# A dynamic convolution in front of a squared-ReLU layer on one core: the short conv form from block 5 instead of block 8

## The chip, the core and the metric

The kernel runs on one core of one Trainium2 chip. The metric is the device time of one launch in microseconds (us). The core has TensorE (PE in the profile; PEld is its weight load), VectorE (DVE), ScalarE (ACT), GpSimd (POOL) and SyncE (SP). Each works through its own list of instructions in order; they wait for each other by semaphores. Transfers (DMA) are issued here from the queues of SyncE and GpSimd.

## The reference

`x` is 8 x 4096 x 192, `weight_gen` 8 x 4096 x 8 x 7 (8 heads, 7 taps). The kernel may take the products in f16.

```
w = exp(weight_gen - max); w = w / sum(w)          # softmax over the 7 taps
y[s, h, :] = sum over k of w[s, h, k] * x_padded[s + k, h, :]   # 24 channels a head
h = maximum(y @ w_in, 0)                            # 192 -> 2048
out = (h * h) @ w_out                               # 2048 -> 192, for 32768 tokens
```

## The kernel before

**Blocks.** The 32768 tokens are 64 stretches of 512. Block 0 and block 1 hold one stretch each, blocks 2 to 32 two each (`BLOCKS`). The text counts blocks from 0 as the code does, so the sixth block is block 5. Each batch of the input is 8 stretches; block 5 is the first block of batch 1.

**What a block needs.** First the softmax weights of its tokens (class `Softmax`: `exp` on ScalarE, L244; sums, reciprocals and products on VectorE, L251, L258, L266). A part of the tokens is done in two to four pieces, each a step "S" in the plan. When a part's last piece is done, its rows are moved by DMA into tiles `wr` that lie by token: `move_rows` straight from SBUF (L361) for small parts, or through a copy `vd` in HBM (L280, then L327). Then VectorE multiplies `wr` with a mask into bands `bd` (L406; a step "B" for one stretch, in one or two instructions). The tokens of `x` come in as `xt` from GpSimd's queue, which also casts them to f16 (L317 to L327).

**The conv** of block j + 1 (step "C", `st_conv`) is a set of small matmuls of `xt` with `bd` into two PSUM tiles `yp`, which are then copied to `y` in SBUF. In the older form (L536) groups of 32 channels are computed in two rounds, since a group reaches over two heads: 120 matmuls, and ScalarE copies 1024 and 512 columns (L547). In the short form (`st_conv_spread`, L502) each head has its own 32 rows, so 80 matmuls are enough. The rows then hold 24 channels of one head, and heads 6 and 7 are brought into the 8 free rows by four DMAs `y<-y` (L516). Here 1024 columns are copied on ScalarE and 1024 on VectorE (L512). The channels of `y` then stand in another order, so `w_in` is needed with its rows in that order: `w_p`, loaded by `load_w_spread` (16 DMAs on GpSimd's queue, which cast) and completed by `cross_w_spread` (2 DMAs).

**The units.** A block has 16 units "u" (`st_unit`, units 0 to 15). One is six matmuls of `w_i` or `w_p` with `y` into a PSUM tile `h` (L581), the relu on ScalarE (L595), and, for two units at once, the square on VectorE (L599; units 14 and 15 one by one).

**The second product.** "M" is one half of a quarter of the block before: 64 matmuls of `g` with `w_o` (L630) into the PSUM tiles `o0` and `o1`, of which there is one each. Every second M ends a quarter: ScalarE copies one (L644), VectorE adds the other (L646), and the next M needs both free.

**The order** is written out by hand, and nothing reorders it: `plans` gives the steps of blocks 0 to 3; from block 4 on a string of steps is used, `steady` up to block 6 and `steady_spread` from block 7 (the block before the first that uses the short form).

```python
steady = "MuMuuu" * 3 + "MuuuMCu"
steady_spread = "MuMuuu" * 2 + "MuCMuuu" + "MuMuuu"
```

Softmax pieces (`TIMES`: block and unit), exps (`exp_time`) and bands (`us`) are put ahead of a unit. In blocks 4, 5 and 6 the two bands of the next block stand ahead of units 7 and 9, 5 and 9, 7 and 9; from block 7 on ahead of 1 and 5.

**Buffers** that bear on this: three PSUM tiles for `h` and `yp` together, three tiles `t` of two units each between ScalarE and VectorE, two `y`, two `xt`, two `o_sb`.

Of the kernel before, what the change touches and what calls it, by code (L numbers as in the profile page):

```python
# [9 lines left out]
def kernel(  # L10
# [26 lines left out]
    nc = tc.nc  # L37
# [7 lines left out]
    HK = H * KK  # L45
    G = D // H
    SPREAD = H - 2
    FIRST_SPREAD = 8
    HP = H // 2

    P = 128
# [11 lines left out]
    RT = 64  # L63
    NK = D // RT
# [34 lines left out]
    FIRST = 8  # L99
# [44 lines left out]
    def load_w_spread():  # L144

        def rows(head, k=None):
            a = moe_w_in[G * head : G * (head + 1)]
            return a if k is None else a.rearrange("(r k) c -> k r c", k=NK)[k]

        for e in (0, 1):  # L150
            for k in range(NK):
                for a, n, src in (
                    (0, G, rows(2 * k + e)), (G, RT // 2 - G, rows(SPREAD + e, k))
                ):
                    if k < 2:
                        p0 = RT * k + 32 * e + a
                        nc.gpsimd.dma_start(
                            out=w_p[p0 : p0 + n, :, 0, 0:NQ],
                            in_=src.rearrange("r (q c) -> r q c", q=WQ),
                        )  # L160
                    else:
                        for half in (0, 1):
                            p0 = RT * half + 32 * e + a
                            nc.gpsimd.dma_start(
                                out=w_p[p0 : p0 + n, :, 0, NQ:],
                                in_=src.rearrange("r (q h c) -> h r q c", q=WQ, h=2)[half],
                            )
    def cross_w_spread():
        for r0, r1 in ((0, RT), (RT, 0)):
            nc.gpsimd.dma_start(out=w_p[r0 : r0 + RT, :, 1], in_=w_p[r1 : r1 + RT, :, 0])  # L170
# [137 lines left out]
    def tile_start(j, i):  # L308

        t1 = (j % NBB + 1) * TB  # L310
        return TB - P if i == NT - 1 and t1 in ends(j // NBB) else starts[i]
# [169 lines left out]
    def st_conv_spread(j):  # L481

        s0, n = BLOCKS[j]
        y = p_y.tile([P, NK + 1, TB], f16, name="y")
        y_t[j] = y
        for ks in ((NK, NK - 1), (0, 1)):
            yp = ps_h.tile([P, 2, TB], f32, name="yp", tag="h")
            k0 = min(ks)
            for k in ks:
                for i in range(NT):  # L490
                    a, b = bounds[i], bounds[i + 1]
                    for half in (0, 1):
                        s = s0 + half
                        hi = a + (STEP if tile_start(s, i) == starts[i] else b - a)
                        bd = bd_t[s][:, H * a : H * hi].rearrange(
                            "p (g c e) -> p g e c", g=HP, e=2
                        )
                        for e in (0, 1):
                            head = 2 * k + e
                            p0 = RT * half + 32 * e  # L500
                            c0 = min(G * head, D - 32)
                            nc.tensor.matmul(  # L502
                                out=yp[p0 : p0 + 32, k - k0, a:b],
                                lhsT=x_t[s][:, i, c0 : c0 + 32],
                                rhs=bd[:, head // 2, e, 0 : b - a],
                                start=True,
                                stop=True,
                                skip_group_check=True,
                                tile_position=(0, p0),
                            )  # L510
            copy = nc.vector.tensor_copy if k0 == 0 else nc.scalar.copy
            copy(out=y[:, k0 : k0 + 2], in_=yp)  # L512
        for p0 in range(0, P, 32):
            head = SPREAD + p0 // 32 % 2
            r0 = p0 + G * head - min(G * head, D - 32)
            nc.sync.dma_start(out=y[p0 + G : p0 + 32, 0:NK], in_=y[r0 : r0 + G, NK])  # L516

    def st_conv(j):

        if j >= FIRST_SPREAD:  # L520
            return st_conv_spread(j)
# [49 lines left out]
    def st_unit(j, u):  # L571

        w = w_p if j >= FIRST_SPREAD else w_i
        h = ps_h.tile([P, 2, TB], f32, name="h", tag="h")
# [91 lines left out]
    with nc.allow_low_precision("fp16 matmul pipeline"), tc.manual_schedule():  # L666

        block_of = {n: j for j, (s, c) in enumerate(BLOCKS) for n in range(s, s + c)}
        parts = []
# [7 lines left out]
        def move_rows(s, engines=(nc.sync, nc.gpsimd)):  # L677

            n = parts.index(s)
            first = s.b * NBB + s.t0 // TB  # L680
            near = [p for p in parts[max(n - 1, 0) : n + 1] if p.b == s.b]
            for j in range(first, first + P * s.r // TB):
                wr_load_sbuf(j, near, range(NT), engines)
# [70 lines left out]


        steady = "MuMuuu" * 3 + "MuuuMCu"
        steady_spread = "MuMuuu" * 2 + "MuCMuuu" + "MuMuuu"
        plans = {
            0: "u B1 u u u E1 C S1 u u M u u",
# [9 lines left out]
        def at(j, u, kind, *args):  # L769
            fill.setdefault((j, u), []).append((kind, *args))  # L770
# [4 lines left out]
        TIMES = {  # L775
            (1, 0): ((3, 15), (4, 0)),
            (1, 1): ((4, 15), (5, 0)),
            (1, 2): ((4, 2), (5, 1), (5, 15)),
            (2, 0): ((6, 1), (6, 15), (7, 0)),
            (2, 1): ((7, 9), (8, 9)),  # L780
            (3, 0): ((9, 9), (10, 0), (10, 9), (11, 9)),
        }

        def exp_time(j, u):

            if u == 0:
                return j - 1, 12
            return j, {1: 0, 2: 1, 7: 3, 8: 4, 9: 4, 13: 12, 15: 8}[u]
# [17 lines left out]
            at(times[0][0] - 1, 0, "L", n)  # L806
        for j in range(len(plans), NBLK - 1):
            a = BLOCKS[j + 1][0]
            small = [p for p in parts if p.fb <= j + 1][-1].r == FIRST
            us = {4: (7, 9), 6: (7, 9)}.get(j, (5, 9) if small else (1, 5))  # L810
            if j + 1 >= FIRST_SPREAD:
                us = (1, 5)
            for n, u in enumerate(us):
                at(j, u, "B", a + n)
        for j in range(len(plans), NBLK):
            plan, u = [], 0
            for step in steady_spread if j + 1 >= FIRST_SPREAD else steady:
                if step == "u":
                    plan += [f"{kind}{n}" for kind, n in fill.get((j, u), ())]
                    u += 1  # L820
                plan.append(step)
            plans[j] = " ".join(plan)
# [14 lines left out]
        def soft(s):  # L837
            lo, hi = next(s.softs)
            s.total(lo, hi)
            s.recip(lo, hi)  # L840
            s.scale(lo, hi, nc.vector)
            if hi < s.rh:
                return
            if s.r == FIRST:
                move_rows(s)
                after = parts[parts.index(s) + 1]
                if after.b == s.b and after.r > FIRST:
                    s.store(nc.sync)
            else:
                s.store(nc.sync)  # L850
                stored.add(s)
                for w in [w for w in waiting if w[0] is s]:
                    waiting.remove(w)
                    load_rows(w[1])
# [21 lines left out]
        for j in range(NBLK):  # L876
            if j + 2 < NBLK:
                load_rows(j + 2)
            if j == 1:
                for q in range(WQ):  # L880
                    cross_w_in(q)
            u = 0
            for step in plans[j].split():
                kind, n = step[0], int(step[1:] or 0)
                if kind == "u":
                    st_unit(j, u)
                    u += 1
                elif kind == "M":
                    next(mm2)
                elif kind == "C" and j + 1 < NBLK:  # L890
                    st_conv(j + 1)
                    if j == 0:
                        x_load(3)
                    elif j + 2 < NBLK:
                        for k in range(BLOCKS[j + 2][0], sum(BLOCKS[j + 2])):
                            x_load(k)
                    if j == 5:
                        load_w_spread()
                    elif j == 6:
                        cross_w_spread()  # L900
                elif kind == "E":
                    parts[n].exp(*next(parts[n].exps))
                elif kind == "S":
                    soft(parts[n])
                elif kind == "B":
                    st_bands(n)
                elif kind == "L":
                    parts[n].load(nc.sync)


        j = NBLK - 1
# [44 lines left out]
```

## Time and profile before

| what | value |
| --- | --- |
| median of 3 runs | 730.38 us (729.42, 730.40, 730.38) |
| profiled execution, span | 728.4 us |
| mean granted TensorE clock | 1.000 |
| VectorE, ScalarE busy | 86%, 84% of the span |
| L581 matmuls, w_i and w_p | 576 and 2400, 376 ns each |
| L536 conv, older form | 6 convs of 120 matmuls |
| L502 conv, short form | 25 convs of 80 matmuls |

The profile is one execution of the program. Its span runs from the first to the last instruction; for the profiled execution no other time is given, and the runs' times lie 1.0 to 2.0 us above the span. Busy time is the time in which an engine works on at least one instruction. Durations of instructions that follow each other on one engine overlap a little, so that the cost of one in a chain is the distance from its start to the next one's. TensorE's work is read best from start to start too, because its ends are modelled.

The stretches between the first M of one block and of the next, from the view of busy time in chosen windows:

| block | from, to (us) | length | VectorE busy | ScalarE busy |
| --- | --- | --- | --- | --- |
| 4 | 73.28, 96.12 | 22.84 | 21.69 | 20.21 |
| 5 | 96.12, 118.69 | 22.57 | 21.21 | 19.38 |
| 6 | 118.69, 141.24 | 22.55 | 19.20 | 20.10 |
| 7 | 141.24, 163.33 | 22.09 | 21.05 | 18.52 |
| 8 | 163.33, 185.43 | 22.10 | 19.83 | 18.88 |

### The profile page before, as it was taken

What the parts mean: (1) busy time and instruction counts of PE and PEld (TensorE: products, weight loads), DVE (VectorE), ACT (ScalarE), POOL (GpSimd) and SP (SyncE); (2) the same over time, 40 slices, a digit from 0 to 9 for tenths busy, and PEclk for the clock granted to TensorE, in tenths of its full rate; (3) what the DMA queues carried; (4) which work ended last, traced back from release to release, by engine and by line L of the source; (5) the groups of instructions that cost most, each with busy time, mean ns of one, the idle gap of its engine ahead of it and who ended that gap; (6) DMA issues with size and microseconds to landing.
All of it is one profiled execution on the core that took longest, in us unless ns stands there. A gap on an engine that the chain in (4) does not pass through costs nothing.

```text
span 728.4 us, 31046 instructions
## 1 busy us (share of the span) xinstructions
PE 722.0 (99%) x14078; PEld 530.1 (73%) x14078; DVE 625.8 (86%) x839; ACT 612.0 (84%) x731; POOL 98.5 (14%) x146
## 2 busy tenths in 40 slices
PE   8999999999999999999999999999999999999998
PEld 5668877777777777777777777777777777777777
DVE  7999997998898998888988888988888988778753
ACT  6998888888888888888888888888888888888883
POOL 7231223411001100011001010010000110001000
PEclk9999999999999999999999999999999999999999
DMA  9664465676245443356432554343544325444112
GB/s 193 128 113 106 82 125 89 128 142 138 78 71 133 99 84 68 75 116 125 83 62 58 135 104 88 66 74 110 114 78 87 57 53 117 67 87 77 30 46 67
DMA packets 126272, 68.30 MB, mean 94 GB/s; under 512 B 85353, under 2 KB 122556, under 8 KB 125628
## 3 DMA queue, kind: packets, MB, share of 16 engines
q0 software_dynamic: 46192, 19.43, 22.9%
q1 hardware_dynamic: 79804, 46.79, 22.5%
q8 instruction: 110, 1.80, 1.1%
q14 instruction: 22, 0.18, 0.1%
q10 hardware_dynamic: 144, 0.10, 0.0%
HBM read 50.18 MB, written 28.70 MB: 108 GB/s over the span
## 4 chain that ended last, share of the span: by engine, by line
PE 98%; DMA 1%; SPq 0%; ACT 0%; issue 0%; ACTq 0%
PE o L630 47%; PE h L581 44%; PE yp L502 4%; PE h L566 2%; PE yp L536 1%; DMA w_st<-in_moe_w_in_dram 1%; SPq L219 0%; PE yp L466 0%; ACT w_i L740 0%; SPq L135 0%; SPq L133 0%; ACT y L476 0%; SPq L327 0%; SPq L317 0%; ACT o_sb L644 0%
## 5 line engine op out<-in xcount | busy, mean ns | idle before, releaser
L595 ACT ACTIVATE t<-h 128x1024 f16<-128x1024 f32 x512 | 496.6, 1027 | 60.1 <-PE h L581 58.4
L630 PEld LDWEIGHTS <-g 64*128 64x128 f16 (+1 forms) x8032 | 344.3, 94 | 55.2 <-issue 2.3
L630 PE MATMUL o<-w_o,g 64*128 64x192 f16 (+1 forms) x8032 | 380.1, 243 | 0.1
L599 DVE TENSOR_TENSOR g<-t 128x2048 f16<-128x2048 f16 (+1 forms) x287 | 307.4, 1105 | 28.7 <-ACT t L595 28.3
L581 PE MATMUL h<-y,w_p 64*128 64x512 f16 x2400 | 291.7, 376 | 0.0
L581 PEld LDWEIGHTS <-w_p 64*128 64x128 f16 x2400 | 113.9, 94 | 94.8
L406 DVE TENSOR_TENSOR bd<-wr,mask 128x4160 f16<-128x4160 f16 (+4 forms) x90 | 149.5, 1685 | 1.2 <-ACT wr L391 1.2
L646 DVE TENSOR_TENSOR o_sb<-o,o_sb 128x384 f32<-128x384 f32 x123 | 68.4, 556 | 61.4 <-ACT o_sb L644 60.3
L327 POOL DMA_DIRECT2D xt<-in_x_dram x63 | 52.6, 838 | 415.4 <-PE yp L502 362.5
L644 ACT COPY o_sb<-o 128x384 f32<-128x384 f32 x129 | 61.6, 477 | 45.7 <-PE o L630 44.4
L581 PE MATMUL h<-y,w_i 64*128 64x512 f16 x576 | 70.5, 376 | 0.0
L581 PEld LDWEIGHTS <-w_i 64*128 64x128 f16 x576 | 30.5, 94 | 21.7 <-issue 1.2
L502 PEld LDWEIGHTS <-xt 128*32 128x32 f16 x2000 | 24.6, 95 | 10.6 <-issue 10.6
L266 DVE TENSOR_TENSOR v_big<-ex,rcp 128x112 f16<-128x112 f32 (+5 forms) x180 | 29.9, 237 | 2.1 <-DMA vd<-v_big 1.1
L512 DVE CAST y<-yp 128x1024 f16<-128x1024 f32 x25 | 30.4, 1218 | 0.0
L502 PE MATMUL yp<-bd,xt 128*32 128x104 f16 (+1 forms) x2000 | 28.4, 210 | 0.0
L244 ACT ACTIVATE ex<-wg 128x560 f32<-128x560 f32 (+5 forms) x40 | 26.3, 659 | 1.2 <-DMA wg<-in_weight_gen_dram 1.2
L251 DVE TENSOR_REDUCE ssum<-ex 128x80 f32<-128x560 f32 (+5 forms) x40 | 25.6, 639 | 1.3 <-ACT ex L244 1.3
L512 ACT CAST y<-yp 128x1024 f16<-128x1024 f32 x25 | 25.2, 1007 | 0.0
L258 DVE RECIPROCAL rcp<-ssum 128x64 f32<-128x64 f32 (+4 forms) x39 | 23.0, 589 | 1.4
L317 POOL DMA_DIRECT2D xt<-in_x_dram x7 | 3.9, 555 | 120.4 <-PE yp L502 109.4
L361 POOL DMA_DIRECT2D wr<-v_first x24 | 13.0, 559 | 24.0 <-DVE v_first L266 23.8
(42 smaller groups left out, 111.9 us busy)
## 6 DMA issues: line engine op xcount, KB each, us to landing
out_dram<-o_sb SPq DMA_DIRECT2D x63, 384.0 KB
xt<-in_x_dram POOLq DMA_DIRECT2D x42, 240.0 KB, 4.9
wg<-in_weight_gen_dram SPq DMA_DIRECT2D x4, 1064.0 KB
xt<-in_x_dram POOLq DMA_DIRECT2D x21, 192.0 KB, 5.0
wr<-vd SPq DMA_DIRECT2D x38, 80.0 KB
vd<-v_big SPq DMA_DIRECT2D x5, 512.0 KB
y<-y SPq DMA_DIRECT2D x100, 24.0 KB
wg<-in_weight_gen_dram SPq DMA_DIRECT2D x3, 616.0 KB
```

The source lines that it names most:

```text
L244: nc.scalar.activation(out=self.ex[:, lo:hi].rearrange("p r g k e -> p (r g) k e"), in_=self.wg[:, lo:hi].rearrange("p r (g e) k -> p (r g ...
L266: eng.tensor_tensor(out=bass.AP(tensor=v.tensor, offset=v.offset + lo * H * SL + lo % SL * 2 + g * SL * 2, ap=[list(v.ap[0]), [H * SL + 2, ...
L327: eng.dma_start(out=dst[:, first:last], in_=ap)
L406: nc.vector.tensor_tensor(out=bd_t[j][:, H * lo : H * (lo + len(tiles) * n)].rearrange("p (g m c) -> p g m c", g=shape[1], c=2 * SL), in0= ...
L502: nc.tensor.matmul(out=yp[p0 : p0 + 32, k - k0, a:b], lhsT=x_t[s][:, i, c0 : c0 + 32], rhs=bd[:, head // 2, e, 0 : b - a], start=True, sto ...
L512: copy(out=y[:, k0 : k0 + 2], in_=yp)
L581: nc.tensor.matmul(out=h[:, half], lhsT=w_in_chunk(w, u, slot, half), rhs=y_t[j][r0 : r0 + RT, k], start=(slot == 0), stop=(slot == NK - 1 ...
L595: nc.scalar.activation(out=t1[:, e], in_=h, func=ActF.Relu)
L599: nc.vector.tensor_tensor(out=g[:, a : e + 1], in0=t1[:, a : e + 1], in1=t1[:, a : e + 1], op=AluOp.mult)
L630: nc.tensor.matmul(out=oo[:, cc * Dm : (cc + 1) * Dm], lhsT=g[r0 : r0 + n, cc * P : (cc + 1) * P], rhs=w_o[r0 : r0 + n, fc, :], start=(fc ...
L644: nc.scalar.copy(out=o_sb, in_=o[0][:, c])
L646: nc.vector.tensor_tensor(out=o_sb, in0=o[1][:, c], in1=o_sb, op=AluOp.add)
```

## The change

The short form is used from block 5 on (`FIRST_SPREAD`), so the convs for blocks 5, 6 and 7 change form. For these (`j < SHARED`) both copies of `yp` are on ScalarE, and two of the four DMAs `y<-y` are issued from GpSimd. Their conv stands in a string of its own, `first_spread`, behind the block's tenth unit; in `steady` it stood behind the fifteenth. The bands of these three blocks stand ahead of units 5 and 7. One softmax piece moves from unit 15 of block 5 to unit 13; its exp stays ahead of unit 8. `load_w_spread` moves from behind the conv of block 5's plan to the softmax piece in block 3, `cross_w_spread` from block 6 to the softmax piece at the start of block 4.

```diff
-    FIRST_SPREAD = 8
+    FIRST_SPREAD = 5
+    SHARED = 8
...
-            copy = nc.vector.tensor_copy if k0 == 0 else nc.scalar.copy
+            copy = nc.vector.tensor_copy if k0 == 0 and j >= SHARED else nc.scalar.copy
             copy(out=y[:, k0 : k0 + 2], in_=yp)
...
-            nc.sync.dma_start(out=y[p0 + G : p0 + 32, 0:NK], in_=y[r0 : r0 + G, NK])
+            eng = nc.gpsimd if j < SHARED and p0 >= RT else nc.sync
+            eng.dma_start(out=y[p0 + G : p0 + 32, 0:NK], in_=y[r0 : r0 + G, NK])
...
         steady = "MuMuuu" * 3 + "MuuuMCu"
+        first_spread = "MuMuuu" * 2 + "MuuCMuu" + "MuMuuu"
...
-            (1, 2): ((4, 2), (5, 1), (5, 15)),
+            (1, 2): ((4, 2), (5, 1), (5, 13)),
...
+            if (j, u) == TIMES[(1, 2)][-1]:
+                return j, 8
...
-            small = [p for p in parts if p.fb <= j + 1][-1].r == FIRST
-            us = {4: (7, 9), 6: (7, 9)}.get(j, (5, 9) if small else (1, 5))
-            if j + 1 >= FIRST_SPREAD:
-                us = (1, 5)
+            us = (5, 7) if FIRST_SPREAD <= j + 1 < SHARED else (1, 5)
...
-            for step in steady_spread if j + 1 >= FIRST_SPREAD else steady:
+            form = steady if j + 1 < FIRST_SPREAD else steady_spread
+            for step in first_spread if FIRST_SPREAD <= j + 1 < SHARED else form:
...
-                    if j == 5:
-                        load_w_spread()
-                    elif j == 6:
-                        cross_w_spread()
...
                 elif kind == "S":
                     soft(parts[n])
+                    if (j, n) == (FIRST_SPREAD - 2, 3):
+                        load_w_spread()
+                    elif (j, n) == (FIRST_SPREAD - 1, 4):
+                        cross_w_spread()
```

## The prediction

> **What bounds the kernel now.** I read the table of busy time, then the chain of waits that ended last, then the timelines of TensorE and VectorE block by block. The first two say that TensorE is never out of work:
>
> ```profile
> PE 722.0 (99%) x14078; PEld 530.1 (73%) x14078; DVE 625.8 (86%) x839; ACT 612.0 (84%) x731; POOL 98.5 (14%) x146
> PE 98%; DMA 1%; SPq 0%; ACT 0%; issue 0%; ACTq 0%
> ```
>
> So a shorter conv on TensorE shortens the span, and a new TensorE wait lengthens it, one for one. TensorE's timeline around the conv for block 5 (old form, L536), then around the conv for block 8 (short form, L502); columns are start, duration, engine, line, operation, count:
>
> ```profile
> 83.75 1.52 PE L630 MATMUL o<-w_o,g 64*128 64x192 f16 x32
> 85.06 0.85 PE L581 MATMUL h<-y,w_i 64*128 64x512 f16 x6
> ...
> 92.24 1.52 PE L630 MATMUL o<-w_o,g 64*128 64x192 f16 x32
> 93.69 1.57 PE L536 MATMUL yp<-bd,xt 128*32 128x104 f16 x120
> 95.20 0.82 PE L581 MATMUL h<-y,w_i 64*128 64x512 f16 x6
> 96.12 1.08 PE L630 MATMUL o<-w_o,g 64*128 64x192 f16 x22
> ```
>
> ```profile
> 153.02 0.81 PE L581 MATMUL h<-y,w_i 64*128 64x512 f16 x6
> 153.76 1.13 PE L502 MATMUL yp<-bd,xt 128*32 128x104 f16 x80
> 154.82 1.49 PE L630 MATMUL o<-w_o,g 64*128 64x192 f16 x32
> ```
>
> Starts give the clean prices: an "M" step 1.31 (83.75 to 85.06), a unit 0.65, the short conv 1.07 plus 0.10 ahead of it. From one block's first M to the next the starts are 73.28, 96.12, 118.69, 141.24, 163.33: blocks 4, 5, 6 take 22.84, 22.57, 22.55 us, block 7, which holds the first short conv, 22.09.
>
> **The gain.** If blocks 4, 5, 6 (which compute the convs for 5, 6, 7) fall to 22.09, that is 0.75 + 0.48 + 0.46 = 1.69 us. The instruction order of the changed kernel confirms 240 rows less on TensorE (three times 40 matmuls and 40 weight loads). Units cost the same with `w_p` as with `w_i` (376 ns a matmul in both groups).
>
> **What moves.** The conv goes from behind the fifteenth unit to behind the tenth: it is asked for three M steps and five units earlier, 3 x 1.31 + 5 x 0.65 = 7.2 us. It needs both bands (L406) of the next block. They move too, but only ahead of one pair's square (1.14) and one `o_sb` add (0.5). VectorE in block 4, before:
>
> ```profile
> 78.71 1.23 DVE L599 TENSOR_TENSOR g<-t 128x2048 f16<-128x2048 f16 x1 [0.73 <-ACT t L595]
> 79.85 0.62 DVE L251 TENSOR_REDUCE ssum<-ex 128x64 f32<-128x448 f32 x1
> 80.50 0.55 DVE L258 RECIPROCAL rcp<-ssum 128x64 f32<-128x64 f32 x1
> 81.16 0.83 DVE L266 TENSOR_TENSOR v_big<-ex,rcp 128x112 f16<-128x112 f32 x4
> 81.91 1.22 DVE L599 TENSOR_TENSOR g<-t 128x2048 f16<-128x2048 f16 x1
> 83.05 0.55 DVE L646 TENSOR_TENSOR o_sb<-o,o_sb 128x384 f32<-128x384 f32 x1
> 83.75 1.23 DVE L599 TENSOR_TENSOR g<-t 128x2048 f16<-128x2048 f16 x1
> 84.89 2.39 DVE L406 TENSOR_TENSOR bd<-wr,mask 128x832 f16<-128x832 f16 x2
> 87.19 1.22 DVE L599 TENSOR_TENSOR g<-t 128x2048 f16<-128x2048 f16 x1
> 88.33 0.55 DVE L646 TENSOR_TENSOR o_sb<-o,o_sb 128x384 f32<-128x384 f32 x1
> 88.80 2.35 DVE L406 TENSOR_TENSOR bd<-wr,mask 128x3328 f16<-128x3328 f16 x2
> 91.06 1.22 DVE L599 TENSOR_TENSOR g<-t 128x2048 f16<-128x2048 f16 x1
> ```
>
> VectorE never rests here after 79; it is behind. The second band ends at 91.05, 2.64 before the conv at 93.69. That cover is smaller than the 7.2 taken away. Prices from start to start: square 1.14, softmax piece of 64 sums 2.06 (79.85 to 81.91; 1.98 in block 5), of 48 sums 1.74, band 2.23 to 2.30, add 0.5.
>
> *Block 4.* Changed order on VectorE: square, softmax piece, square, add, band, square, band. From 78.71: 1.14 + 2.06 + 1.14 + 0.50 = 83.55; + 2.30 = 85.85; + 1.14 = 86.99; the second band's large part lasts to 88.87, its last tile to 89.25. TensorE arrives at 83.75 + 1.31 + 2 x 0.65 + 0.10 = 86.46. It waits to 88.95 and 0.25 more inside for the last tile: **2.7**. The conv ends at 90.26.
>
> *Block 5.* First M at 90.26 + 3.95 + 6 x 0.65 = 98.1. VectorE, no longer behind, now waits for its units: the relu of unit 13 ends at 98.07. Then square 99.24, square of unit 14 99.84, softmax piece 101.82, square of unit 15 102.42, softmax piece 104.16, add to 104.7. The add frees the output bank that the third M needs at 98.1 + 5.24 = 103.34 (the second M needs unit 15's square, and stands for the same time): **1.4**. On VectorE: piece 106.6, two squares 108.9, add 109.4, band 111.6, square 112.75, band 115.0 (large part 114.6). TensorE arrives at 104.75 + 7.93 = 112.7: **2.3** with the inner wait.
>
> *Block 6.* First M at 123.85; its second M ends at 127.14, add to 128.4, softmax piece with its wait for the stored `v_big` (1.13 before, 0.6 here) to 131.0, squares 133.3, add 133.9, band 136.1, square 137.25, band 139.5. TensorE arrives at 137.0: **2.6**.
>
> *Block 7.* The same two softmax pieces around its start as in block 5: **1.4**. Its bands stand at units 1 and 5 as before, and end at 162.3, just before TensorE at 162.45. From there the rest runs as before.
>
> *Both evictions on ScalarE* (1.01 each; before 1.01 and 0.59 on it). In a stalled conv they lie in the wait's shadow: nothing. Without the stall, two relus, two evictions and the copy put the `o_sb` add at the seventh M's need or 0.5 past it; that is a rival below. In blocks 4, 5 and 6 ScalarE is busy 20.2, 19.4 and 20.1 us, VectorE 21.7, 21.2 and 19.2, so where VectorE is late the eviction's 1.22 is better off it. The Trainium skill (TensorEngine Tiling (Array Packing), PSUM Bottleneck) says the opposite, to use both engines for evacuation; by it one of each conv's evictions would go back to VectorE, and with the rows above that makes the 8.7 larger, not smaller, wherever VectorE is the late one.
>
> *Permuted weights.* 16 loads of some 0.58 us on GpSimd's queue, in block 3 instead of 5 (120.16 to 132.56 before, 3.2 of it waits). Behind them stand four `xt` loads and four `wr` moves. From 62.0 they end near 73; `xt` is then issued at 75 to 78 instead of 73 to 75.6, lands 5 us later (median 4.9), 83 against a need of 88.9. `wr` is issued at 78 to 80, as before. `w_p<-w_p` goes at 81, lands 7.3 later, 88; needed at 99. All hidden: nothing. If the cover went, `xt` some 8 us late would add up to 2.5 in block 4. The moved softmax piece (unit 13 instead of 15) fills idle VectorE time: nothing.
>
> *y over two queues.* SyncE's four issues last 2.83, so two of them save about 1.4 of latency, with some 7 us between conv and first use: nothing.
>
> **Sum.** Stalls 2.7 + 1.4 + 2.3 + 2.6 + 1.4 = 10.4; gain 1.69; net +8.7. The profiled execution's span is 728.4, the runs' median 730.38 lies 2.0 above it, and I carry that difference over: 739.1. Uncertain: restarting after a wait may cost more than the 0.1 I took. The only such stop is at 96.12, where the add ended at 95.62 and the M was due at 95.86, so 0 to 0.27 each, 1.4 for five. Below: should the two bank stalls be hidden (2.8) and two convs wait 0.5 less, 735.3. Above: 1.4 and the late `xt` 2.5 give 743.0.
>
> The clock was granted at 1.00 in every block read. The Trainium skill (TensorE: Matmul & The Clock Gate, What's actually happening) says that an idle window of about 3.4 us halves the clock until about 3.4 us of work have passed. My longest wait is 2.7, so by it nothing; were three waits to trip it, an estimate from that page is three times 1.7, 5.1 more, 744. No TensorE wait that long is in this trace.
>
> **Rivals.**
> 1. *Bands in time.* VectorE is 2.5 us or more faster to the second band, all three convs run unhindered, 730.38 - 1.69 = 728.7. For it: 86% busy on average is not full. Against it: in blocks 4 and 5 it is busy 21.7 and 21.2 us, and every item ahead of the band is in the order. It decides at the second band: done by 86.5 or not.
> 2. *ScalarE's evictions become the wait.* Bands in time, but the add is 0.5 late at the seventh M, three times: 728.7 + 1.6 = 730.3, no change.
> 3. *Only the first conv stalls*, since the stall lets VectorE catch up: 730.38 + 2.7 - 1.7 = 731.4. For it: VectorE has idle time after each early conv. Against: the softmax pieces of block 5 come after that idle time and before its bands.
> 4. *Transfers late as well*, weights ahead of `xt` and `wr` on one queue, or longer waits: 743 to 748.
>
> **Chances.** Forecast, with its sizes from 735 to 743.5: 0.76. Rival 1: 0.06. Rival 2: 0.03. Rival 3: 0.05 at 731.4, and 0.03 up to 735. Rival 4: 0.07. A measurement of this kernel can tell 0.2% (1.5 us) from no change; faster is rival 1, same rivals 2 and 3. Range 735 to 743.5.
>
> **What would show it.** Right: in TensorE's timeline gaps of 2 to 3 us ahead of the first three L502 groups, ended by VectorE's bands; smaller ones at the second or third M of blocks 5 and 7; afterwards blocks of 22.1. Wrong: the conv for block 5 starting near 86.5, the waits ended by a DMA, or a granted clock under 1.00. The size is wrong if VectorE's order or its prices differ from those rows.

## The result and the profile after

The changed kernel takes 740.88 us (median of 740.04, 741.54, 740.23 and 745.38), the kernel before 730.17 (four runs beside it). The ratio is 1.0162, 95% interval 1.0144 to 1.0179: slower. The profiled execution took 740.04, its span is 738.3 against 728.4, the mean granted clock 0.998. All times of day below are us from the start of the span of the kernel named. The changed kernel's lines lie a little lower: the short conv is L503, the older form L538, a unit L583, M L632, the square L601, the relu L597, the bands L407, the `o_sb` copy L646 and add L648, the copies of `yp` L513, the `y<-y` DMAs L518.

The page of the kernel after: busy time, the chain of waits, and two groups (busy, mean ns of one, then the idle time ahead and what ended it):

```profile
PE 724.0 (98%) x13958; PEld 530.6 (72%) x13958; DVE 625.9 (85%) x839; ACT 613.9 (83%) x731; POOL 101.2 (14%) x152
...
PE o L632 40%; PE h L583 37%; PE yp L503 4%; DVE bd L407 1%; DVE g L601 1%; ACT t L597 0%; DVE v_big L267 0%; ACT o_sb L646 0%; DVE rcp L259 0%; DVE o_sb L648 0%; DVE ssum L252 0%
...
L632 PE MATMUL o<-w_o,g 64*128 64x192 f16 (+1 forms) x8032 | 381.8, 243 | 2.4 <-DVE g L601 2.3
...
L503 PE MATMUL yp<-bd,xt 128*32 128x104 f16 (+1 forms) x2240 | 33.3, 211 | 6.1 <-DVE bd L407 5.9
```

(An M is 32 matmuls, as the lines show; the 64 given above are those of a whole quarter.) TensorE has 120 matmuls less and yet is busy 2.0 us longer. VectorE stands in the chain now, with the bands and the squares. The idle time of TensorE is in two rows: 5.9 us ahead of the conv, ended by bands, and 2.3 ahead of M, ended by squares. TensorE's timeline of the kernel after, around the four places that the prediction named (in brackets the idle time ahead and what ended it):

```profile
84.81 1.51 PE L583 MATMUL h<-y,w_i 64*128 64x512 f16 x12
86.25 0.22 PE L503 MATMUL yp<-bd,xt 128*32 128x104 f16 x2
88.63 1.39 PE L503 MATMUL yp<-bd,xt 128*32 128x104 f16 x78 [2.15 <-DVE bd L407]
89.94 1.50 PE L632 MATMUL o<-w_o,g 64*128 64x192 f16 x32
...
99.77 1.34 PE L632 MATMUL o<-w_o,g 64*128 64x192 f16 x28
102.25 0.34 PE L632 MATMUL o<-w_o,g 64*128 64x192 f16 x4 [1.15 <-DVE g L601]
...
112.31 0.22 PE L503 MATMUL yp<-bd,xt 128*32 128x104 f16 x2
114.25 1.87 PE L503 MATMUL yp<-bd,xt 128*32 128x104 f16 x78 [1.72 <-DVE bd L407]
116.05 2.58 PE L632 MATMUL o<-w_o,g 64*128 64x192 f16 x32
118.47 1.46 PE L583 MATMUL h<-y,w_p 64*128 64x512 f16 x12
...
138.42 0.22 PE L503 MATMUL yp<-bd,xt 128*32 128x104 f16 x2
140.69 1.14 PE L503 MATMUL yp<-bd,xt 128*32 128x104 f16 x78 [2.04 <-DVE bd L407]
...
154.06 0.34 PE L632 MATMUL o<-w_o,g 64*128 64x192 f16 x4 [1.15 <-DVE g L601]
...
163.47 1.14 PE L503 MATMUL yp<-bd,xt 128*32 128x104 f16 x80
```

Each of the three early convs starts with two matmuls on the first band and then stands for the second; the conv at 163.47, in block 7, runs through. The second M of blocks 5 and 7 stands 1.15 for unit 15's square. One more thing is to be seen at 116.05: the M behind the conv lasts 2.42 to the next start, where the one behind block 4's conv takes 1.34. VectorE's timeline of the kernel after shows why the first conv stands, and, from 99.53 on, why the second M of block 5 does:

```profile
83.25 2.38 DVE L407 TENSOR_TENSOR bd<-wr,mask 128x832 f16<-128x832 f16 x2
85.56 1.22 DVE L601 TENSOR_TENSOR g<-t 128x2048 f16<-128x2048 f16 x1
86.69 2.35 DVE L407 TENSOR_TENSOR bd<-wr,mask 128x3328 f16<-128x3328 f16 x2
...
99.53 0.61 DVE L252 TENSOR_REDUCE ssum<-ex 128x64 f32<-128x448 f32 x1
100.17 0.55 DVE L259 RECIPROCAL rcp<-ssum 128x64 f32<-128x64 f32 x1
100.76 0.83 DVE L267 TENSOR_TENSOR v_first<-ex,rcp 128x112 f16<-128x112 f32 x4
101.51 0.68 DVE L601 TENSOR_TENSOR g<-t 128x1024 f16<-128x1024 f16 x1
```

There is no idle time in the first three: TensorE asks at 86.25, while VectorE is on a square, and the second band's large part runs from 86.69 to 88.57, its small part to 89.04. In block 5 a softmax piece lies ahead of unit 15's square, which ends at 102.19; the M goes on at 102.25.

From first M to first M the blocks take:

| block | before | after | difference | forecast |
| --- | --- | --- | --- | --- |
| 4 | 22.84 | 24.77 | +1.93 | +1.95 |
| 5 | 22.57 | 27.20 | +4.63 | +3.22 |
| 6 | 22.55 | 24.61 | +2.06 | +2.14 |
| 7 | 22.09 | 23.43 | +1.34 | +1.40 |
| sum | 90.05 | 100.01 | +9.96 | +8.71 |

The four blocks hold the whole difference of the spans, 9.9. Only block 5 is off the forecast, by 1.4. The view of busy time in chosen windows of the kernel after (window, length, busy time of TensorE, its weight load, VectorE, ScalarE and GpSimd with instructions, then the granted clock, the DMA share and GB/s) says by what:

```profile
112.30:114.20 1.90, 0.23 (x4) 0.10 (x3) 1.90 (x3) 1.41 (x2) 0.00 (x0) 1.00 0.87 306
114.20:116.05 1.85, 1.70 (x78) 1.42 (x77) 1.85 (x3) 0.74 (x1) 0.00 (x0) 0.70 0.01 2
116.05:118.50 2.45, 2.45 (x38) 2.28 (x36) 0.89 (x1) 1.18 (x2) 0.98 (x2) 0.53 0.03 7
118.50:121.00 2.50, 2.50 (x46) 1.75 (x42) 0.56 (x1) 2.15 (x3) 2.01 (x3) 1.00 0.40 52
```

Behind the wait the clock was granted at 0.70 and 0.53, then at 1.00 again. Clock lost: (1 - 0.70) x 1.85 + (1 - 0.53) x 2.45 = 1.7 us, one stretch of 3.4 us at half. The conv there took 1.80 where block 4's took 1.31, the M behind it 2.42 where block 4's took 1.34: 1.57 more. The runs' times follow the same thing: clocks of 0.998, 0.999, 0.995 and 0.993 go with 740.04, 740.23, 741.54 and 745.38.

### The profile page after: what moved, and what is told of

It reads as the page before. It is cut to its first block, busy times and chain, and to the rows that moved or that the text cites. A ratio compares the mean times of both kernels' runs of the same rounds, so it can differ in the third digit from the quotient of the medians.

```text
span 738.3 us, 30840 instructions
## 1 busy us (share of the span) xinstructions
PE 724.0 (98%) x13958; PEld 530.6 (72%) x13958; DVE 625.9 (85%) x839; ACT 613.9 (83%) x731; POOL 101.2 (14%) x152
## 4 chain that ended last, share of the span: by engine, by line
PE 81%; DVE 2%; ACT 0%; issue 0%
PE o L632 40%; PE h L583 37%; PE yp L503 4%; DVE bd L407 1%; DVE g L601 1%; ACT t L597 0%; DVE v_big L267 0%; ACT o_sb L646 0%; DVE rcp L259 0%; DVE o_sb L648 0%; DVE ssum L252 0%
## 5 line engine op out<-in xcount | busy, mean ns | idle before, releaser
L597 ACT ACTIVATE t<-h 128x1024 f16<-128x1024 f32 x512 | 496.5, 1026 | 60.2 <-PE h L583 58.6
L632 PEld LDWEIGHTS <-g 64*128 64x128 f16 (+1 forms) x8032 | 344.8, 94 | 57.8 <-DVE g L601 3.0
L632 PE MATMUL o<-w_o,g 64*128 64x192 f16 (+1 forms) x8032 | 381.8, 243 | 2.4 <-DVE g L601 2.3
L601 DVE TENSOR_TENSOR g<-t 128x2048 f16<-128x2048 f16 (+1 forms) x287 | 307.5, 1105 | 33.9 <-ACT t L597 33.8
L583 PE MATMUL h<-y,w_p 64*128 64x512 f16 x2688 | 326.8, 376 | 0.0
L583 PEld LDWEIGHTS <-w_p 64*128 64x128 f16 x2688 | 128.0, 94 | 105.8
L407 DVE TENSOR_TENSOR bd<-wr,mask 128x4160 f16<-128x4160 f16 (+4 forms) x90 | 149.4, 1685 | 0.7 <-ACT wr L392 0.7
L648 DVE TENSOR_TENSOR o_sb<-o,o_sb 128x384 f32<-128x384 f32 x123 | 68.4, 556 | 67.2 <-ACT o_sb L646 61.9
L646 ACT COPY o_sb<-o 128x384 f32<-128x384 f32 x129 | 61.6, 478 | 49.9 <-PE o L632 49.1
L503 PEld LDWEIGHTS <-xt 128*32 128x32 f16 x2240 | 28.3, 96 | 18.6 <-issue 18.6
L503 PE MATMUL yp<-bd,xt 128*32 128x104 f16 (+1 forms) x2240 | 33.3, 211 | 6.1 <-DVE bd L407 5.9
L583 PE MATMUL h<-y,w_i 64*128 64x512 f16 x288 | 35.4, 376 | 0.0
L513 ACT CAST y<-yp 128x1024 f16<-128x1024 f32 x31 | 30.9, 1008 | 5.1 <-PE yp L503 5.1
L513 DVE CAST y<-yp 128x1024 f16<-128x1024 f32 x25 | 30.4, 1217 | 0.0
L583 PEld LDWEIGHTS <-w_i 64*128 64x128 f16 x288 | 16.5, 94 | 10.5 <-issue 1.2
```

Of the source, the lines that this page charges most:

```text
L407: nc.vector.tensor_tensor(out=bd_t[j][:, H * lo : H * (lo + len(tiles) * n)].rearrange("p (g m c) -> p g m c", g=shape[1], c=2 * SL), in0= ...
L503: nc.tensor.matmul(out=yp[p0 : p0 + 32, k - k0, a:b], lhsT=x_t[s][:, i, c0 : c0 + 32], rhs=bd[:, head // 2, e, 0 : b - a], start=True, sto ...
L583: nc.tensor.matmul(out=h[:, half], lhsT=w_in_chunk(w, u, slot, half), rhs=y_t[j][r0 : r0 + RT, k], start=(slot == 0), stop=(slot == NK - 1 ...
L597: nc.scalar.activation(out=t1[:, e], in_=h, func=ActF.Relu)
L601: nc.vector.tensor_tensor(out=g[:, a : e + 1], in0=t1[:, a : e + 1], in1=t1[:, a : e + 1], op=AluOp.mult)
L632: nc.tensor.matmul(out=oo[:, cc * Dm : (cc + 1) * Dm], lhsT=g[r0 : r0 + n, cc * P : (cc + 1) * P], rhs=w_o[r0 : r0 + n, fc, :], start=(fc ...
```

## The experiments

**Theory.** The conv's place makes the loss: behind the tenth unit it meets VectorE on the second band, and two softmax pieces hold up the squares at the starts of blocks 5 and 7. The 40 matmuls saved per conv come through, but are smaller. **Rivals:** the new form or the permuted weights cost time themselves; both copies of `yp` on ScalarE or the second DMA queue do; or the gain would not appear even with the bands on time, because the next step waits in the conv's place. Each run was made beside runs of the kernel before, 729.98 to 730.20 in the median; the ratios are to those.

### The form put back, the place kept: old_form

```diff
-        if j >= FIRST_SPREAD:
+        if j >= SHARED:
...
-        w = w_p if j >= FIRST_SPREAD else w_i
+        w = w_p if j >= SHARED else w_i
```

> The place of the conv and of the bands as in the change; the convs for blocks 5 to 7 and their units in the older form (120 matmuls, w_i, no y transfers). Theory: the same waits for the bands, plus the longer conv, about 0.5 us three times, so 741.5 to 742.5. Rival (the short form with its evictions or weights costs the time): back to 730 to 732.

742.93 us, ratio 1.0177 (1.0143 to 1.0210), 0.4 above what was expected. The waits are those of the change, with 120 matmuls behind them (TensorE's timeline):

```profile
88.17 2.87 PE L538 MATMUL yp<-bd,xt 128*32 128x104 f16 x118 [2.17 <-DVE bd L407]
...
115.47 1.86 PE L538 MATMUL yp<-bd,xt 128*32 128x104 f16 x118 [1.72 <-DVE bd L407]
```

So the loss belongs to the place. What the short form gains beside it isn't clear of noise in the times: 2.0 in the medians, 1.1 by the ratios, whose intervals overlap, and the clock differs from run to run. Here the half clock came with the first wait: 2.87 for a conv that takes 1.57. Block 6 had the full clock in both profiled executions, and there the gain can be read: 25.05 from first M to first M in old_form, 24.61 in the change, 0.44 less where 0.46 was worked out.

### The place put back, the form kept: old_place

```diff
-        first_spread = "MuMuuu" * 2 + "MuuCMuu" + "MuMuuu"
+        first_spread = "MuMuuu" * 3 + "MuuuMCu"
...
-            us = (5, 7) if FIRST_SPREAD <= j + 1 < SHARED else (1, 5)
+            us = {4: (7, 9), 5: (5, 9), 6: (7, 9)}.get(j, (1, 5))
```

> Short form, evictions, weights and y transfers as in the change; only the conv of blocks 4 to 6 goes back behind the fifteenth unit and the bands back to units 7 and 9 (5 and 9 in block 5). Theory (the conv overtook its bands): the waits of 2.2 to 2.7 us ahead of the three convs go, but y is ready only some 4.5 us after the conv (in the changed kernel the conv ends at 89.94, the second eviction at 91.52, the last y transfer is issued at 92.4 and lands 2.0 later), while the next block's unit 0 asks for it 1.96 after the conv: a new wait of about 2.5 us three times. 730.2 - 1.7 + 7.5 = 736.0, and TensorE's gaps stand behind the next block's first M. Rival (form, evictions on ScalarE or the early weights cost the time): place does not matter, 740 to 741, with gaps still ahead of the convs.

750.55 us, ratio 1.0272 (1.0245 to 1.0299): 14.5 over what was expected. The half that it was made for held: the convs run without a wait. But the short form has the step that the older one lacks, `y<-y` by DMA, and one unit is no room for it. TensorE's timeline at the start of blocks 5, 6 and 7:

```profile
99.41 0.82 PE L583 MATMUL h<-y,w_p 64*128 64x512 f16 x6 [2.45 <-DMA y<-y]
...
132.90 1.46 PE L583 MATMUL h<-y,w_p 64*128 64x512 f16 x6 [8.22 <-DMA y<-y]
...
160.06 0.37 PE L583 MATMUL h<-y,w_p 64*128 64x512 f16 x1 [2.31 <-DMA y<-y]
```

The first is the latency that had been expected, and so is the third, with 1.26 more behind its first matmul. The 8.22 is another thing, and SyncE's queue in the same trace shows a part of it:

```profile
121.02 0.32 SPq L281 DMA_DIRECT2D vd<-v_big  x1
125.32 0.94 SPq L328 DMA_DIRECT2D wr<-vd  x2
126.35 0.48 SPq L653 DMA_DIRECT2D out_dram<-o_sb  x1
126.92 1.54 SPq L518 DMA_DIRECT2D y<-y  x2
```

The softmax part is stored at 121.02, its reload by token waits for that store until 125.32, and `y<-y` is issued behind it, at 126.92, 3.85 after GpSimd's two. The DMA that waits holds what is behind it in its queue. The last of SyncE's two then lands 5.0 us after its issue, where GpSimd's last took 2.0 (what made it slow isn't shown). The rest is clock: its mean was 0.988, five stretches of 3.4 us at half, three of them in a row from within the 8.22 on:

```profile
132.70:136.50 3.80, 3.60 (x36) 2.87 (x38) 0.00 (x0) 1.02 (x1) 0.00 (x0) 0.50 0.37 140
```

TensorE's waits in these blocks are 2.45, 1.11 (an add ahead of the 8.22), 8.22, 2.31 and 1.26, 15.35 in all and 7.85 over the 7.5 expected; its work took 5.7 longer at half clock (1.67, 2.44 and 1.57 behind the three waits). 736.0 + 7.85 + 5.7 = 749.6. So the early place of the conv isn't arbitrary: the form needs several us between the conv and its first unit.

### The cause moved both ways: bands_5_5 and bands_7_9

Only the place of the two bands in VectorE's order changes: both ahead of unit 5 (one square earlier for the second), or ahead of units 7 and 9 (one square later for each).

```diff
-            us = (5, 7) if FIRST_SPREAD <= j + 1 < SHARED else (1, 5)
+            us = (5, 5) if FIRST_SPREAD <= j + 1 < SHARED else (1, 5)
```

> As the change, but both bands stand ahead of unit 5, so that the second no longer lies behind the square of units 4 and 5 (1.14 us on VectorE). Theory: each of the three waits ahead of the convs is 1.1 us shorter, 3.4 in all: 737.0 to 737.5, and 1.5 less again if the half-clock window after the conv for block 6 goes with it. Rival (waits not on VectorE's order): 740 to 741.

> As the change, but the bands stand ahead of units 7 and 9, one square later each: the suspected wait is made longer. Theory: about 1.1 us more in each wait, 3.4 in all, so 744; if waits of nearly 4 us bring half-clock windows, 1.5 us for each more, up to 749, and the granted clock falls below that of the changed kernel. Rival: no change, 740 to 741.

bands_5_5: 736.28 us, ratio 1.0079 (1.0054 to 1.0105). bands_7_9: 749.05 us, 1.0250 (1.0223 to 1.0278). TensorE's timeline, the first conv of each:

```profile
88.94 1.38 PE L503 MATMUL yp<-bd,xt 128*32 128x104 f16 x78 [1.07 <-DVE bd L407]
```

```profile
90.55 2.02 PE L503 MATMUL yp<-bd,xt 128*32 128x104 f16 x78 [3.55 <-DVE bd L407]
```

One square (1.14) earlier takes 1.1 off each conv's wait (2.15, 1.72 and 2.04 become 1.07, 0.58 and 0.91). The sum 3.35, and the half-clock stretch of 1.6 that is gone too (the mean clock is 1.000), are 4.9 against 4.6 in the medians. One square later adds 1.4 to 1.8 to each, where 1.1 was expected, and there are four stretches at half clock (mean 0.991): 749.05 lies at the upper end of what was expected. VectorE's order ahead of the conv is what the time follows.

### What the copies and the second queue do: split_evict

```diff
-            copy = nc.vector.tensor_copy if k0 == 0 and j >= SHARED else nc.scalar.copy
+            copy = nc.vector.tensor_copy if k0 == 0 else nc.scalar.copy
...
-            eng = nc.gpsimd if j < SHARED and p0 >= RT else nc.sync
+            eng = nc.sync
```

> As the change, but the convs for blocks 5 to 7 are evicted like the later ones (one half on VectorE, one on ScalarE) and all four y transfers go from SyncE. Theory: VectorE is idle for some 4 us behind each early conv (0.67, 1.56, 1.24 and 0.66 us in block 4), so the 1.22 us eviction fits there and the waits ahead of the convs stay: 740 to 741.5. Rival (both evictions on ScalarE cost the time): 736 to 738. If VectorE were short of time behind the convs too: 743.

742.21 us, 0.7 above what was expected, ratio 1.0158 (1.0138 to 1.0177), against the change's 1.0162 (1.0144 to 1.0179): no difference (of the two together; they weren't run apart). The waits are the same to 0.02, and the clock is not: the profiled execution has two half-clock stretches, behind the first and the second conv, with a mean of 0.995, and another run, 739.93, has 1.000.

### The conv two units later: conv_12

```diff
-        first_spread = "MuMuuu" * 2 + "MuuCMuu" + "MuMuuu"
+        first_spread = "MuMuuu" * 2 + "MuuMuuC" + "MuMuuu"
```

> As the change, but the conv stands behind the twelfth unit, 2.6 us of TensorE work later. Theory: the waits ahead of the convs nearly go, but VectorE runs the sixth M's add behind bands and two squares, so the seventh M, which follows the conv at once, waits for it: 1.6 to 1.9 us instead of 2.7 in block 4 and much the same in 5 and 6; 737.5 to 738.5, waits ended by L648. Rival (only the bands matter, nothing behind them): 733.

735.76 us, ratio 1.0082 (1.0066 to 1.0098). The conv doesn't wait any more, the M behind it does:

```profile
88.86 1.19 PE L503 MATMUL yp<-bd,xt 128*32 128x104 f16 x80
...
91.83 1.48 PE L632 MATMUL o<-w_o,g 64*128 64x192 f16 x31 [1.59 <-DVE o_sb L648]
```

The output bank is freed by VectorE's add, which stands behind two squares, and these behind the bands. The wait went from one step to the next on the same engine's list; it is shorter than expected (1.59, 1.16, 1.01 in the three blocks), and the time lies 1.7 below the range.

### The softmax pieces moved out of the way: soft_bands, tuned_13

The pieces ahead of unit 15 and unit 0 go to units 10 and 12 of blocks 4 and 6; the bands stand as in bands_5_5.

```diff
-            (1, 1): ((4, 15), (5, 0)),
+            (1, 1): ((4, 10), (4, 12)),
...
-            (2, 0): ((6, 1), (6, 15), (7, 0)),
+            (2, 0): ((6, 1), (6, 10), (6, 12)),
```

> As bands_5_5 (736.3), and the softmax pieces that stood around the starts of blocks 5 and 7 are done in VectorE's idle time behind the convs of blocks 4 and 6 (ahead of units 10 and 12). Theory: the two waits of 1.15 us at the second M of blocks 5 and 7 go, 2.3 to 2.8 less: 733.5 to 734, and no TensorE wait for a square is left there. Rival (those waits are not the softmax pieces' doing): 736.

734.39 us, ratio 1.0065 (1.0047 to 1.0083), 0.4 above what was expected. The two waits of 1.15 at the second M are gone; the waits that the view has for these blocks are now the convs' alone, 1.37, 0.42 and 0.91 (2.7 in all):

```profile
PE yp L503 <- DVE bd L407: 2.7, 3, 1.4
```

tuned_13 put the conv behind the thirteenth unit, the second band ahead of unit 10, and the pieces at unit 12 and unit 0 of the next block:

```diff
+        first_spread = "MuMuuu" * 2 + "MuuMuuMuC" + "Muuu"
...
+            us = {4: (5, 10), 5: (5, 10), 6: (7, 10)}.get(j, (1, 5))
```

> Conv behind the thirteenth unit, bands ahead of units 5 and 10 (7 and 10 in block 6), first softmax piece ahead of unit 12 in blocks 4 and 6. Theory: 0.5 to 0.9 us of wait for the second band, some 0.2 at the seventh M, y landing just in time (4.5 us after the conv, asked for after 4.6), so 1 us a block against a gain of 1.69 in all: 731 to 732.5; at best, with y and bands both in time, 729. Rival (the short form in blocks 5 to 7 costs time wherever the conv stands): 735 and more.

735.98 us, ratio 1.0084 (1.0066 to 1.0103); a miss, as high as its rival had it. But it isn't the form that costs it: no conv waits, and two other steps do (view of waits):

```profile
PE o L632 <- DVE o_sb L648: 2.3, 3, 1.0
...
PE h L583 <- DMA y<-y: 1.9, 1, 1.9
```

The adds at the seventh M are late by 0.96, 0.43 and 0.93, and once `y` is not there for unit 0. So the conv is held from both sides: earlier it meets the bands, later the DMA.

### VectorE's work taken away: one_band, pool_squares

one_band is soft_bands with one band computed per block; the convs of blocks 5 to 7 use the first stretch's band for both stretches. pool_squares is soft_bands with the conv behind the twelfth unit and the squares of units 4 to 7 of blocks 4 to 6 on GpSimd.

```diff
+                        sb = s0 if j < SHARED else s
...
+            us = (5,) if FIRST_SPREAD <= j + 1 < SHARED else (1, 5)
```

```diff
+            eng = nc.gpsimd if FIRST_SPREAD <= j + 1 < SHARED and u in (5, 7) else nc.vector
+            eng.tensor_tensor(
```

> As soft_bands (734.4), but the second band of blocks 5, 6 and 7 is left out and the conv uses the first stretch's band for both halves, so that the output of these blocks is not the reference's; the same matmuls, evictions and transfers otherwise. Theory: with 2.3 us less on VectorE ahead of each of the three convs no wait is left there, the seventh M's add is done in time too, and the short form's gain is all that remains: 730.0 - 1.7 = 728.3, to 729. Rival (something else in the change costs time, such as transfers or both evictions on ScalarE): 731 and more.

> As soft_bands, with the conv behind the twelfth unit and the squares of units 4 to 7 of blocks 4, 5 and 6 on GpSimd, which does little else there. Theory: the bands end before the conv asks, and the sixth M's add, no longer behind these squares, before the seventh M asks: the whole gain, 728.5 to 729.5, if GpSimd's square of 128x2048 takes no more than some 4.5 us each (no run shows it yet) and VectorE keeps its pace beside it. Rival (VectorE slows down beside GpSimd, or GpSimd is too slow and holds the tiles t and the y transfers): 731 to 735.

one_band: 730.96 us (10 runs), ratio 1.0011 (1.0001 to 1.0020), 2.0 above the upper end of what was expected. The waits for bands are gone, as they must be, and still nothing is gained. TensorE's timeline of one_band, then ScalarE's and VectorE's, at the same place:

```profile
86.66 1.19 PE L504 MATMUL yp<-bd,xt 128*32 128x104 f16 x80
87.78 1.49 PE L633 MATMUL o<-w_o,g 64*128 64x192 f16 x32
89.11 1.46 PE L584 MATMUL h<-y,w_i 64*128 64x512 f16 x12
...
91.31 1.48 PE L633 MATMUL o<-w_o,g 64*128 64x192 f16 x31 [0.35 <-DVE o_sb L649]
```

```profile
88.35 1.94 ACT L514 CAST y<-yp 128x1024 f16<-128x1024 f32 x2
90.14 0.52 ACT L647 COPY o_sb<-o 128x384 f32<-128x384 f32 x1
```

```profile
90.70 0.56 DVE L649 TENSOR_TENSOR o_sb<-o,o_sb 128x384 f32<-128x384 f32 x1 [0.98 <-ACT o_sb L647]
```

The conv takes 1.12, as the price had it. But between the sixth M and the seventh stand two units, where the older order has three. ScalarE copies `yp` twice, then the bank at 90.14; VectorE, idle for 0.98, adds at 90.70; and the M that was due at 89.11 + 2 x 0.65 = 90.41 runs from 91.31. That is 0.90, and with the other two blocks (0.48 and 0.87, worked out in the same way) 2.25: more than the 1.69 that the form saves. Over blocks 4 to 7 it takes 91.08 against 90.05 before.

pool_squares: 751.98 us, ratio 1.0288 (1.0272 to 1.0305), 22.5 to 23.5 over what was expected. GpSimd's and VectorE's timelines of it:

```profile
83.58 8.99 POOL L602 TENSOR_TENSOR g<-t 128x2048 f16<-128x2048 f16 x2 [2.94 <-ACT t L597]
```

```profile
83.32 11.46 DVE L407 TENSOR_TENSOR bd<-wr,mask 128x832 f16<-128x832 f16 x4
94.71 1.21 DVE L602 TENSOR_TENSOR g<-t 128x2048 f16<-128x2048 f16 x1
```

GpSimd takes 4.5 for a square here, and 3.8 to 5.7 over all six. While it is on two of them, VectorE's two bands last 11.46, where the kernel after needs 2.38 + 2.35: their large parts take 5.29 each, 1.88 in the kernel after, and their small ones no longer than there. The square behind them, after GpSimd is done, takes its 1.21 again. The convs then wait 5.26, and 1.39 + 3.49 in the next block, and the mean clock falls to 0.986, some 10 us of clock lost.

### One unit more ahead of the seventh M: one_band_uuu, soft_bands_uuu

```diff
-        first_spread = "MuMuuu" * 2 + "MuuCMuu" + "MuMuuu"
+        first_spread = "MuMuuu" * 2 + "MuuCMuuu" + "MMuuu"
```

> As the kernel with one band (the second band of blocks 5 to 7 is left out, so their output is not the reference's), but with three units instead of two between the sixth and the seventh M of blocks 4 to 6, and none between the seventh and the eighth. Theory (what eats the gain once the bands are in time is the add at the seventh M: ScalarE copies yp twice, 88.35 to 90.29, then the output bank, 90.14, VectorE adds at 90.70, and the bulk of the M starts at 91.31 where it was due at 89.11 + 2 x 0.65 = 90.41, 0.90 late in each of three blocks): one unit more is 0.65 of cover each, 730.96 - 3 x 0.65 = 729.0, and no wait of a seventh M over 0.3. Rival (ScalarE and VectorE are full in these blocks, and the time comes back as a wait of a unit or of the next block's first M): 731 or more.

> The complete kernel with the early softmax pieces and both bands ahead of unit 5, and the same shift of one unit ahead of the seventh M. Theory: its three conv waits (1.37, 0.42, 0.91) stay; its seventh M in block 4 was due at 90.86 + 2 x 0.65 = 92.16 and its bulk started at 92.54, 0.38 late, so three times 0.4 to 0.65 goes: 734.39 less 1.2 to 1.9 is 732.5 to 733.2. Rival (the time comes back elsewhere): 734.4 or more.

soft_bands_uuu: 732.84 us, ratio 1.0039 (1.0025 to 1.0053): the cheapest complete version, as expected, and still slower than the kernel before. one_band_uuu: 730.75 us (11 runs), 1.0008 (1.0000 to 1.0017): 1.7 over what was expected, 0.25 under the rival's 731, and no different from one_band. By the waits the rival was right: the seventh M doesn't wait any more, and the next block's first M does, behind the softmax piece that VectorE has just ahead of the add (TensorE, then VectorE):

```profile
97.17 1.48 PE L633 MATMUL o<-w_o,g 64*128 64x192 f16 x31 [0.47 <-DVE o_sb L649]
```

```profile
95.94 0.71 DVE L267 TENSOR_TENSOR v_first<-ex,rcp 128x84 f16<-128x84 f32 x4
96.57 0.55 DVE L649 TENSOR_TENSOR o_sb<-o,o_sb 128x384 f32<-128x384 f32 x1
```

In this profile 0.65 of the span more than in one_band's arises ahead of block 4 already, where the two orders are the same; by blocks 4 to 7 alone it is 90.64 against one_band's 91.08 and 90.05 before.

## Why the prediction was right, point by point

**The bound, the gain.** Right. TensorE's idle time appears one for one in the blocks' lengths. Of the gain, block 6 of old_form against the change shows 0.44 where 0.46 was worked out; the whole 1.69 is not clear of noise in the times.

**The three conv waits.** Right in mechanism, place and engine; each a little too large. From the ask to the next step, less the 1.12 of one_band's conv, which doesn't wait: block 4 2.57 (forecast 2.7), block 5 2.62 with the clock's 0.49 in it, so 2.1 (2.3), block 6 2.22 (2.6). bands_5_5 and bands_7_9 show that it is VectorE's order. "VectorE never rests" was the decisive reading, and the start-to-start prices of square, band and softmax piece carried the sum.

**The two stops of 1.4.** Right: from start to next step 99.77 to 102.43 and 151.58 to 154.24, 2.66 each, less 1.31: 1.35. The second M stood, for unit 15's square, as the bracket in the prediction has it. soft_bands took them away by moving the softmax pieces.

**Block 7's bands in time; permuted weights, `xt` and `wr` hidden.** Right: the conv at 163.47 and the first unit on `w_p` run without a wait (99.12, ahead of the 99.77 shown).

**Copies on ScalarE: nothing; two queues: nothing.** Right for this kernel (split_evict). The reason given, the wait's shadow, fits: in the kernel after the add behind the two copies ends at 92.54, and the seventh M starts at 92.57. On the Trainium skill's rule (TensorEngine Tiling (Array Packing), PSUM Bottleneck: use both engines), the measurement finds neither gain nor loss, 742.21 against 740.88 with intervals that cover each other; the prediction's remark that it would enlarge the loss isn't shown.

**The clock: the term that was mis-sized.** "My longest wait is 2.7, so by it nothing" was wrong by 1.6 us in the profiled execution (1.57 more in the conv at 114.25 and the M behind it). Half the clock was taken for 3.4 us after a wait of 1.72, and not after the waits of 2.15 and 2.04 of the same execution. The Trainium skill (TensorE: Matmul & The Clock Gate, What's actually happening) gives an idle window of about 3.4 us as the condition; the run shows that much less can do. The size of the loss (half the speed for 3.4 us) agrees with that page. It makes the profiled 740.04 out of some 738.5. The four times less what their mean clocks lose (740.04 at 0.998 less 1.5) are, by this estimate, 737.8 to 740.2, so the clock can account for the 1.8 by which the median lies above 739.1. That the number came so near has some luck in it: the three conv waits were priced 0.7 too long in sum, and the clock at nothing.

**The rivals.** 1 (bands in time) and 3 (only the first conv stands): no, three stood. 4 (transfers late as well): no wait in the kernel after is ended by a DMA at these places. 2 (the copies on ScalarE delay the add at the seventh M) is not seen in the change, since the bands stand in front of it. It lies right behind: with one band it is there, 0.90, 0.48 and 0.87 where 0.5 had been priced, and in conv_12 and tuned_13 the same step waits because VectorE is late. This answers where the gain went: the short form saves 1.69 on TensorE, and the order that it needs has 2.25 of waiting in it even when the bands are on time.

**What stays open.** Why the clock fell after 1.72 and not after 2.15; in split_evict three like waits went with two half-clock stretches in the profiled execution, and another run of the same kernel had a mean clock of 1.000. Whether a version exists that keeps the 1.69: of the twelve variants none is faster than before.

## What to carry to other kernels

When a step on the full engine is moved earlier, take the units of time that it loses in cover and set them against the list of the engine that feeds it, item by item, at start-to-start prices: here 7.2 us of cover were taken and 2.6 had been spare. Where that engine is behind, a wait that is taken from one step comes back at the next one that it feeds, so price the second wait before counting a gain. Each stop of the full engine also risks the clock: in the two profiled executions with one half-clock stretch of 3.4 us it cost 1.57 (the kernel after) and 1.2 (old_form) on top.

## What the runs showed of the hardware

- The granted clock of TensorE went to half for 3.4 us at a wait of 1.72 us in the kernel after and at one of 2.17 in old_form, but not at 2.15 and 2.04 in the kernel after. Profiled executions without a wait over 1.6 us (bands_5_5, conv_12, soft_bands) had a mean of 1.000. Two other runs of soft_bands, and one of the kernel before (733.50 us), had 0.998, so a length of wait that is safe isn't shown.
- VectorE's f16 multiplies of two tensors took 11.46 us instead of 4.7, with GpSimd multiplying two tensors in 8.99 of them; 2.4 times as long, all of it in the two large pieces (5.29 each instead of 1.88). What the two share isn't shown.
- A DMA in SyncE's queue that waits for another's landing held the `y<-y` issues behind it for 3.85 us; these then took 5.0 to land instead of 2.0, and TensorE stood 8.22 us for them instead of some 2.4.
